# Attention and MLP on one core: weights loaded up to four pieces ahead, first loads dealt out over two queues, and every later q transposed by DMA

## The chip, the cores and the metric

The kernel runs on one core of a Trainium2 chip. The metric is device time in microseconds (us) for one execution; lower is better. The engines of the core are called PE (TensorE, matmul), PEld (its weight loads), DVE (VectorE), ACT (ScalarE), POOL (GpSimd) and SP (SyncE, which here only issues DMAs; "SPq" and "ACTq" are the queues on which SP and ACT issue them).

## The reference

```python
# q, k, v: (batch 8, heads 8, seq 576, head_dim 64) float32; tau = 0.02
scores = (q @ k.transpose(0, 1, 3, 2)) / sqrt(64)
scores = where(scores >= max(scores, -1) - tau, scores, -1e9)
attn   = softmax(scores, -1)
x      = (attn @ v).transpose(0, 2, 1, 3).reshape(4608, 512)
h      = x @ w_in            # w_in  512 x 2048
out    = (h - tanh(h)) @ w_out   # w_out 2048 x 512
```

## The kernel before

Heads are worked two at a time. There are 32 pairs, four for each of the 8 batches, and a pair has nine score tiles of 128 rows, so there are 288 tiles. The two heads have 576 rows each; eight tiles have 128 rows of one head, and one tile ("shared") has the last 64 rows of both heads.

Preparation of a pair. `load` (L138) brings k, q and v into `raw` tiles, two DMAs each, all issued on SP. `split` (L181), three POOL instructions (L184, L187, L188), scales a float32 tile and writes it as an fp16 high part and an fp16 low part into `hl`. `turn` (L243) transposes `hl`: nine PE transposes (L235) into a PSUM tile of the two-buffer pool `ps_big`, then one DVE copy (L258) to SBUF. For k, POOL also writes a copy with the two halves swapped (`kS`, L264). For q of some pairs, those for which `q_by_dma` (L239) is true, a DMA transpose issued on SP (L247) does this instead. Before the change these are the pairs from 8 on, except the first of each batch.

A tile. `scores` (L303) makes four matmuls (eight on the shared tile) into `ps_big`; DVE scales them and takes the row maximum (L336, L348); ACT writes `z`, which is zero or hugely negative (L363). Then `z` must be transposed. Up to pair 5 PE does it (L382); from pair 6 on, once per two tiles, a DMA transpose issued on SP does (L370, `zT<-z`). ACT takes the exponential (L391 or L399, `pT`), and PE multiplies with v (`attend`, L420, L427, L438). DVE normalizes, PE transposes the result (`emit_x`), and so the MLP's input `xT` is made.

The MLP of a batch (`layers`, L554) is cut into steps of four matmuls: `psH` (L493) for the first product and `psY` (L519) for the second. These steps are dealt out among the tiles of the next batch. The last batches' steps run alone at the end, from about 456 us on.

Weights. The two matrices come in 16 pieces of 512 KB. `w_load` (L629) issues a DMA on SP into a `wt` tile, and `w_cast` (L625) lets POOL write it as bf16 (L627). The pool `wt` has two buffers, so a load waits until the piece two before it has been cast.

Order. The program is written out by hand: one loop over steps `s`, in which scores run eight tiles ahead of `s`, `z` five tiles ahead, and `plan` holds at which step each preparation is put. Each engine, and SP's queue too, runs its own instructions in the order in which the loop wrote them. So an instruction that waits on SP holds up every DMA behind it. In `plan`, a pair whose q goes by DMA has its two splits two steps earlier (L663), and its q transpose seven steps before the pair's first scores, where the PE way has it two or three steps before (L665).

The start. `load_first` (L155) brings k and q of pair 0 in three DMAs each: first head, shared rows, second head. All of k goes on SP, all of q on ACT. `split_first` and `turn_first` work on the first head and the shared rows first (part 0), and on the second head after that (part 1).

Of the kernel before, what the change touches and what calls it, by code (L numbers as in the profile page):

```python
# [9 lines left out]
F32 = mybir.dt.float32  # L10
# [8 lines left out]
def kernel(  # L19
# [11 lines left out]
    nc = tc.nc  # L31
    P = 128

    B, H, S, D = q.shape
# [11 lines left out]
    HPAIR = H // 2  # L46
# [16 lines left out]
    AHEAD = 8  # L63
# [35 lines left out]
    for i in range(6):  # L99
# [8 lines left out]
    pool = lambda name, bufs, **kw: ctx.enter_context(  # L108
        tc.tile_pool(name=name, bufs=bufs, **kw)
    )  # L110
    PSUM = bass.MemoryType.PSUM
    raw_pool = pool("raw", 2)
# [5 lines left out]
    zt_pool = pool("zt", 6)  # L118
    p_pool = pool("p", 3)
    o_pool = pool("o", 2)  # L120
    wt_pool = pool("wt", 2)
    g_pool = pool("g", 2)
    t_pool = pool("t", 3)
    y_pool = pool("y", 2)
# [9 lines left out]
    raws = {}  # L134
# [17 lines left out]
        else:  # L152
            eng.dma_start(out=r[:, 4, :], in_=rem)

    def load_first(t, eng):  # L155

        src = {"k": k, "q": q}[t]
        r = raws[0, t] = raw_pool.tile([P, 10, D], F32, name=f"{t}raw", tag=t)
        for h in range(2):
            eng.dma_start(  # L160
                out=r[:, 5 * h : 5 * h + 4, :].rearrange("p c d -> p (c d)"),
                in_=src[0, h, 0:512, :].rearrange("(p c) d -> p (c d)", c=4),
            )
            if h == 0:
                rem = src[0, 0:2, 512:S, :].rearrange("h s d -> s h d")
                eng.dma_start(out=r[:, 4, :], in_=rem)

    load_first("k", nc.sync)
    load_first("q", nc.scalar)
    warm = const.tile([P, 1], F32, name="warm")  # L170
    nc.vector.memset(warm, 0.0)
    nc.scalar.activation(out=warm, in_=warm, func=ACT.Exp)
# [65 lines left out]

    def q_by_dma(p):  # L239

        return p >= 2 * HPAIR and p % 4 != 0

    def turn(p, t):  # L243
        hl = hls.pop((p, t))
# [58 lines left out]
    def scores(i):  # L303
        p, hh, t = place(i)
        qT, kT, kS = mats[p, "q"], mats[p, "k"], mats[p, "ks"]
        ps = ps_big.tile([P, 1024], F32, name="psS", tag="big")
        main, rem, lo = slice(0, 512), slice(512, 576), 0
        if kind(i) == "B":
            main, rem, lo = slice(512, 1024), slice(448, 512), 448
        if hh is None:  # L310
            qrem = REM
            if q_by_dma(p):
                qrem = (slice(512, 640, 2), slice(513, 640, 2))
            for n, kk in enumerate((kT, kS)):
                for dst, srcs in ((main, MAIN), (rem, REM)):
                    for hh in range(2):
                        nc.tensor.matmul(
                            out=ps[64 * hh : 64 * hh + 64, dst],
                            lhsT=qT[:, qrem[hh]], rhs=kk[:, srcs[hh]],
                            start=(n == 0), stop=(n == 1),  # L320
                        )
        else:
            lhs = qT[:, (5 * hh + t) * P : (5 * hh + t + 1) * P]
            for n, kk in enumerate((kT, kS)):
                for dst, src in ((main, MAIN[hh]), (rem, REM[hh])):
                    nc.tensor.matmul(  # L326
                        out=ps[:, dst], lhsT=lhs, rhs=kk[:, src],
                        start=(n == 0), stop=(n == 1),
                    )
        sc = sc_pool.tile([P, S], F32, name="sc")  # L330
        if kind(i) == "B":
            mx = mxs[i] = mxs.pop(i - 1)
        else:
            mx = mxs[i] = mx3[i // 2 % len(mx3)]
        c = int(kind(i) == "B")
        nc.vector.tensor_scalar(  # L336
            out=sc, in0=ps[:, lo : lo + S], scalar1=SC, scalar2=None,
            op0=ALU.mult, op1=ALU.max, accum_out=mx[:, c : c + 1],
        )
        scs[i] = sc  # L340

    def shift(i):

        if kind(i) == "A":
            return
        mx = mxs.pop(i)
        nb = st_pool.tile([P, 9], F32, name="nb", tag="nb")
        nc.vector.tensor_scalar(  # L348
            out=nb.rearrange("p (a b) -> p a b", b=3)[:, :, 0:2],
            in0=mx.rearrange("p (a b) -> p a b", b=4)[:, :, 0:3],  # L350
            scalar1=-1.0, scalar2=tau, op0=ALU.mult, op1=ALU.add,
        )
        nbs[i - 1], nbs[i] = nb[:, 0:1], nb[:, 1:2]
# [148 lines left out]
    def bend():  # L502
        while halves:
            m, n, ps = halves.pop(0)
            th = t_pool.tile([P, MB], F32, name="th")
            nc.scalar.activation(out=th, in_=ps, func=ACT.Tanh)  # L506
            ths.append((m, n, ps, th))

    def shrink():
        while ths:  # L510
            m, n, ps, th = ths.pop(0)
            nc.vector.scalar_tensor_tensor(  # L512
                out=gs[m][:, n, :], in0=th, scalar=-1.0, in1=ps,
                op0=ALU.mult, op1=ALU.add,
            )
# [98 lines left out]
    def w_pieces():  # L614
        for w, sb, n in ((moe_w_in, w_in_sb, DM_C), (moe_w_out, w_out_sb, DF_C)):
            flat = sb.rearrange("p c n -> p (c n)")
            cols = n * w.shape[1] // 8
            src = w.rearrange("(c p) n -> p c n", p=P)

            for i in (0, 2, 4, 6, 1, 3, 5, 7) if w is moe_w_in else range(8):  # L620
                yield flat, src, i, cols, w.shape[1]

    loaded = []

    def w_cast():  # L625
        flat, wt, i, cols = loaded.pop(0)
        nc.gpsimd.tensor_copy(out=flat[:, i * cols : (i + 1) * cols], in_=wt)  # L627

    def w_load(piece):  # L629
        flat, src, i, cols, width = piece  # L630
        wt = wt_pool.tile([P, cols], F32, name="wt", tag="wt")
        if cols >= width:
            r = cols // width
            s = src[:, i * r : (i + 1) * r, :]
            nc.sync.dma_start(out=wt.rearrange("p (c n) -> p c n", n=width), in_=s)
        else:
            r = width // cols
            s = src[:, i // r, (i % r) * cols : (i % r + 1) * cols]
            nc.sync.dma_start(out=wt, in_=s)
        loaded.append((flat, wt, i, cols))  # L640
# [13 lines left out]
    for p in range(1, NPAIR):  # L654
        first = TPP * p - AHEAD
        for d, f in PREP[3 if p == 1 else 0 :]:
            d -= p == 1 and d in (3, 5)
            if d in (7, 8) and q_by_dma(p):
                d = d + 2
            if p in (2, 4):  # L660
                d = {8: 9, 7: 8, 5: 6}.get(d, d)
            elif d == 5 and p >= 5:
                d = 6 if p % 2 else 3  # L663
            plan.setdefault(first - d, []).append(lambda p=p, f=f: f(p))
        d = 7 if q_by_dma(p) else 3 - (p == 1 or p >= 5)  # L665
        d = 4 if p in (2, 4) else d
# [10 lines left out]
    for t in ("k", "q", "v"):  # L677
        load(1, t)
    pieces = w_pieces()
    w_when = [3, 11, 19, 27] + [4 * i + 32 for i in range(4)] + [3 * i + 47 for i in range(9)]  # L680

    todo, stage = [], 0
    fold = const.tile([P, 64], BF16, name="fold")
# [13 lines left out]
    for s in range(-AHEAD, NTILE + LAG + 3):  # L697
        p, j = divmod(max(s, 0), TPP)
        if 0 <= s < NTILE and j == 2 + LAG and p % HPAIR == 0 and p >= HPAIR:
            assert not todo  # L700
            todo = layers(stage, False)
            share = len(todo) / (HPAIR * TPP - 2 - LAG)
            done, stage = 0.0, stage + 1
        if s == NTILE:
            todo = layers(stage, True)
            share, done, stage = 1, 0.0, stage + 1
        if 0 <= s + AHEAD - 1 < NTILE:
            shift(s + AHEAD - 1)
        if 0 <= s + AHEAD < NTILE:
            scores(s + AHEAD)  # L710
        if s == 1 - AHEAD:
            for t in ("k", "q", "ks"):
                turn_first(t, 1)
        for i in kinks.pop(s, []):
            kink(i)
        bend()
        for i in wts.pop(s, []):
            weights(i)
        if 0 <= s < NTILE + FIRST:
            if todo:  # L720
                done += share
                if s < NTILE and j == TPP - 1 and p % HPAIR == HPAIR - 1:
                    done = 1e9
                while todo and done >= 1:
                    todo.pop(0)()
                    done -= 1
        if s == 0:
            nc.vector.tensor_tensor(
                out=fold, in0=ident_bf[:, 0:64], in1=ident_bf[:, 64:P], op=ALU.add
            )  # L730
        shrink()
        for store in stores[:-1]:
            store()
        del stores[:-1]
        for i in atts.pop(s, []):
            pp, jj = divmod(i, TPP)
            if i < NTILE:
                attend(i)
                odd = pp % 2
                if jj == 3 + odd:  # L740
                    norm(pp, 0)
                elif odd and jj in (0, 8):
                    norm(pp - (jj == 0), 1)
            if pp and jj == 1 + pp % 2:
                emit_x(pp - 1)
        for step in plan.pop(s, []):
            step()
        if True:
            if s + AHEAD in w_when:
                if loaded:  # L750
                    w_cast()
                piece = next(pieces, None)
                if piece:
                    w_load(piece)

    for step in todo:
        step()
# [51 lines left out]
```

## Time and profile before

| What | us |
|---|---|
| Time, median of 6 runs (533.87 to 536.44) | 535.01 |
| The profiled execution's own time | 534.98 |
| Its span, first to last instruction | 533.2 |
| PE busy in the span | 510.2 (96%) |
| ACT busy | 435.4 (82%) |
| DVE busy | 420.5 (79%) |
| POOL busy | 289.7 (54%) |

Busy time is the time in which at least one instruction of that engine was running; an engine that waits is not busy. A share over the whole span hides that the stages differ: the first 100 us load the weights beside the attention, the middle is the same for each batch, and the last 75 us are matmuls alone. A DMA transpose issued on SP takes SP some 1.3 us to issue and lands a median of 3.3 us (`qT`) or 3.6 us (`zT`, 3.2 to 7.6) after its issue began.

### The profile page before, as it was taken

The numbers are of one execution on the slowest core, as the hardware profiler recorded it, in microseconds if no ns is written. First come the engines' busy times: TensorE is split into PE (matmuls) and PEld (weight loads), VectorE is DVE, ScalarE is ACT, GpSimd is POOL, SyncE is SP. The second block draws the span as 40 slices with busy tenths as digits, with TensorE's granted clock in tenths as the row PEclk, the third lists the DMA queues.
The fourth block names the chain that finished last, engine by engine and source line by source line (L and its number), as shares of the span: only waits on it lengthen the run. The fifth ranks groups of instructions, "written<-read, shape, count | busy, mean of one in ns | idle before, by whom it ended". The sixth has DMA issues, their size and how long they took to land.

```text
span 533.2 us, 12716 instructions
## 1 busy us (share of the span) xinstructions
PE 510.2 (96%) x4606; PEld 287.8 (54%) x4606; DVE 420.5 (79%) x1179; ACT 435.4 (82%) x617; POOL 289.7 (54%) x390
## 2 busy tenths in 40 slices
PE   8999899987999999999999999999999999999996
PEld 4666566554556555555555555655555555444444
DVE  5899879995888988898889988898889887554440
ACT  5999899987898999889898989898889999543330
POOL 7999987773755757475727574575747530000000
PEclk9999999997999999999999999999999999999999
DMA  7462767989997999899998899899989996400113
GB/s 202 146 191 88 223 197 146 223 172 192 175 200 158 188 190 203 189 177 199 186 212 170 186 195 193 175 180 196 209 185 178 201 152 109 105 28 33 39 39 81
DMA packets 208607, 86.79 MB, mean 163 GB/s; under 512 B 176160, under 2 KB 200992, under 8 KB 208544
## 3 DMA queue, kind: packets, MB, share of 16 engines
q1 hardware_dynamic: 207952, 85.56, 76.1%
q8 instruction: 36, 0.59, 0.5%
q10 hardware_dynamic: 592, 0.43, 0.3%
q14 instruction: 27, 0.22, 0.1%
HBM read 36.70 MB, written 9.44 MB: 87 GB/s over the span
## 4 chain that ended last, share of the span: by engine, by line
PE 35%; issue 19%; POOL 19%; ACT 10%; DMA 9%; DVE 5%; SPq 2%; POOLq 0%; ACTq 0%; DVEq 0%
PE psY L519 12%; PE psH L493 9%; PE psS L326 6%; POOL kS L264 5%; ACT z L363 4%; ACT pT L391 3%; DMA vraw<-in_v_dram 3%; POOL khl L188 3%; DMA kraw<-in_k_dram 3%; PE psHt L493 3%; DMA zT<-z 2%; POOL vb L216 2%; ACT pT L399 2%; PE psO L427 1%; POOL kraw L184 1%
## 5 line engine op out<-in xcount | busy, mean ns | idle before, releaser
L336 DVE TENSOR_SCALAR_CACHE_REDUCE sc<-psS 128x576 f32<-128x576 f32 x288 | 214.0, 752 | 40.8 <-PE psS L326 24.5
L363 ACT ACTIVATE z<-sc,nb 128x576 bf16<-128x576 f32 x288 | 215.6, 769 | 21.6 <-DVE nb L348 19.4
L399 ACT ACTIVATE pT<-zT 128x1152 f16<-128x1152 bf16 x117 | 135.0, 1154 | 15.3 <-DMA zT<-z 15.2
L519 PE MATMUL psY<-w_out_sb,g 128*128 128x512 bf16 (+1 forms) x592 | 146.3, 374 | 0.8 <-DVE yo L532 0.8
L264 POOL COPY kS<-kT 64x1152 f16<-64x1152 f16 x62 | 70.8, 1142 | 117.6 <-DVE nb L348 115.9
L493 PE MATMUL psH<-xT,w_in_sb 128*128 128x512 bf16 x480 | 124.2, 381 | 2.3 <-DVE g L512 2.3
L326 PEld LDWEIGHTS <-qT 128*128 128x128 f16 x1024 | 75.0, 98 | 61.9 <-issue 7.8
L326 PE MATMUL psS<-kT,qT 128*128 128x512 f16 (+1 forms) x512 | 104.9, 286 | 3.0 <-DVE sc L336 1.5
L326 PE MATMUL psS<-kS,qT 128*128 128x512 f16 x496 | 101.9, 287 | 1.6 <-POOL kS L264 1.5
L512 DVE SCALAR_TENSOR_TENSOR g<-th,psH 128x512 bf16<-128x512 f32 x128 | 87.5, 683 | 19.7 <-ACT th L506 19.1
L506 ACT ACTIVATE th<-psH 128x512 f32<-128x512 f32 x128 | 74.6, 583 | 22.3 <-PE psH L493 21.8
L519 PEld LDWEIGHTS <-g 128*128 128x128 bf16 x592 | 51.1, 98 | 57.3 <-issue 3.2
L493 PEld LDWEIGHTS <-w_in_sb 128*128 128x128 bf16 x576 | 49.3, 98 | 57.5 <-issue 5.5
L427 PE MATMUL psO<-vb,pT 128*128 128x65 bf16 x1024 | 53.5, 194 | 0.0
L427 PEld LDWEIGHTS <-pT 128*128 128x128 f16 x1024 | 44.4, 98 | 9.7
L188 POOL TENSOR_TENSOR qhl<-qraw,qhl 128x576 f16<-128x576 f32 x31 | 39.7, 1279 | 2.7
L188 POOL TENSOR_TENSOR khl<-kraw,khl 128x576 f16<-128x576 f32 x31 | 39.6, 1278 | 2.7
L391 ACT ACTIVATE pT<-psZ 128x512 f16<-128x512 bf16 (+1 forms) x54 | 35.1, 653 | 3.9 <-PE psZ L382 3.6
L532 DVE COPY yo<-psY 128x512 f32<-128x512 f32 (+1 forms) x31 | 21.1, 682 | 14.4 <-PE psY L519 12.7
L420 PE MATMUL psO<-vb,pT 128*128 128x130 bf16 x128 | 28.3, 221 | 4.2 <-ACT pT L399 3.5
L453 DVE TENSOR_TENSOR osb<-psO,rc 128x256 bf16<-128x256 f32 x64 | 27.2, 424 | 2.2
L258 DVE COPY kT<-ps_k 128x1152 f16<-128x1152 f16 x31 | 23.3, 751 | 4.1 <-PE ps_k L235 4.1
(79 smaller groups left out, 507.6 us busy)
## 6 DMA issues: line engine op xcount, KB each, us to landing
vraw<-in_v_dram SPq DMA_DIRECT2D x32, 256.0 KB, 4.2
out_dram<-yo SPq DMA_DIRECT2D x32, 256.0 KB, 2.8
kraw<-in_k_dram SPq DMA_DIRECT2D x31, 256.0 KB, 3.1
qraw<-in_q_dram SPq DMA_DIRECT2D x31, 256.0 KB, 3.6
wt<-in_moe_w_in_dram SPq DMA_DIRECT2D x8, 512.0 KB, 4.3
wt<-in_moe_w_out_dram SPq DMA_DIRECT2D x8, 512.0 KB, 4.7
zT<-z SPq DMA_TRANSPOSE x117, 3.6
kraw<-in_k_dram SPq DMA_DIRECT2D x32, 32.0 KB, 2.9
```

The costliest lines, as they stand in the source:

```text
L188: nc.gpsimd.tensor_tensor(out=hl[:, :, 1, :], in0=x, in1=hl[:, :, 0, :], op=ALU.subtract)
L264: nc.gpsimd.tensor_copy(out=o, in_=i)
L326: nc.tensor.matmul(out=ps[:, dst], lhsT=lhs, rhs=kk[:, src], start=(n == 0), stop=(n == 1),)
L336: nc.vector.tensor_scalar(out=sc, in0=ps[:, lo : lo + S], scalar1=SC, scalar2=None, op0=ALU.mult, op1=ALU.max, accum_out=mx[:, c : c + 1],)
L363: nc.scalar.activation(out=z, in_=sc, func=ACT.Prelu, bias=nb, scale=1.0, alpha=STEEP)
L391: nc.scalar.activation(out=pt[:, off * P : (off + n) * P], in_=ps[:, 0 : n * P], func=ACT.Exp)
L399: nc.scalar.activation(out=pt[:, 0 : n * P], in_=zts.pop(i)[:, 0:n, :], func=ACT.Exp)
L427: nc.tensor.matmul(out=po[:, t - 1 + ab, :], lhsT=pt[:, blk * P : (blk + 1) * P], rhs=vb[:, hh, c, :], start=False, stop=(n == 7), skip_gr ...
L493: nc.tensor.matmul(out=ps, lhsT=w_in_sb[:, c, n * P : (n + 1) * P], rhs=xs[m][:, c, :] if m < B else xR[:, c, :, :], start=(c == 0), stop= ...
L506: nc.scalar.activation(out=th, in_=ps, func=ACT.Tanh)
L512: nc.vector.scalar_tensor_tensor(out=gs[m][:, n, :], in0=th, scalar=-1.0, in1=ps, op0=ALU.mult, op1=ALU.add,)
L519: nc.tensor.matmul(out=ps, lhsT=gs[m][:, n, ms * P : (ms + 1) * P], rhs=w_out_sb[:, n, cols], start=(n == 0), stop=(n == DF_C - 1),)
```

## The change

There are three edits. The pool `wt` gets four buffers, and the steps at which a piece is loaded are separated from those at which one is cast: the casts stay where they were, and the loads come up to four pieces ahead of them. The loads of pair 0 are dealt out over SP and ACT in another order: SP issues k's first head, q's shared rows and k's second head; ACT issues k's shared rows, q's first head and q's second head. And `q_by_dma` is true for every pair from 8 on, so that q of pairs 8, 12, 16, 20, 24 and 28 goes by DMA too; with that, `plan` puts their splits two steps earlier and their transposes five steps earlier than the PE way had it.

```diff
-    wt_pool = pool("wt", 2)
+    wt_pool = pool("wt", 4)
...
-    def load_first(t, eng):
+    def load_first(t, h, eng):
 
         src = {"k": k, "q": q}[t]
-        r = raws[0, t] = raw_pool.tile([P, 10, D], F32, name=f"{t}raw", tag=t)
-        for h in range(2):
+        if (0, t) not in raws:
+            raws[0, t] = raw_pool.tile([P, 10, D], F32, name=f"{t}raw", tag=t)
+        r = raws[0, t]
+        if h is None:
+            rem = src[0, 0:2, 512:S, :].rearrange("h s d -> s h d")
+            eng.dma_start(out=r[:, 4, :], in_=rem)
+        else:
             eng.dma_start(
                 out=r[:, 5 * h : 5 * h + 4, :].rearrange("p c d -> p (c d)"),
                 in_=src[0, h, 0:512, :].rearrange("(p c) d -> p (c d)", c=4),
             )
-            if h == 0:
-                rem = src[0, 0:2, 512:S, :].rearrange("h s d -> s h d")
-                eng.dma_start(out=r[:, 4, :], in_=rem)
-
-    load_first("k", nc.sync)
-    load_first("q", nc.scalar)
+
+
+    for t, h in (("k", 0), ("q", None), ("k", 1)):
+        load_first(t, h, nc.sync)
+    for t, h in (("k", None), ("q", 0), ("q", 1)):
+        load_first(t, h, nc.scalar)
...
     def q_by_dma(p):
 
-        return p >= 2 * HPAIR and p % 4 != 0
+        return p >= 2 * HPAIR
...
-    w_when = [3, 11, 19, 27] + [4 * i + 32 for i in range(4)] + [3 * i + 47 for i in range(9)]
+    load_when = [3, 8, 13, 18, 21, 25, 29, 34, 38, 42, 46, 49, 52, 55, 58, 61]
+    cast_when = [11, 19, 27] + [4 * i + 32 for i in range(3)] + [3 * i + 44 for i in range(10)]
...
-        if True:
-            if s + AHEAD in w_when:
-                if loaded:
-                    w_cast()
-                piece = next(pieces, None)
-                if piece:
-                    w_load(piece)
+        if s + AHEAD in cast_when:
+            w_cast()
+        if s + AHEAD in load_when:
+            w_load(next(pieces))
```

## The prediction, made before the changed kernel was run

> **What bounds the kernel now.** I read the page's busy totals first, and then the table of stretches, for totals hide that stages differ. Its columns: stretch, length, busy time of PE, PEld, DVE, ACT and POOL (instructions in brackets), granted PE clock, DMA share, GB/s.
>
> ```profile
> 115.00:118.00 3.00, 3.00 (x41) 1.65 (x39) 2.13 (x8) 2.93 (x4) 2.06 (x4) 1.00 0.94 196
> 118.00:121.00 3.00, 1.11 (x8) 0.44 (x6) 2.38 (x9) 0.00 (x0) 2.57 (x3) 1.00 1.00 201
> 121.00:124.00 3.00, 1.35 (x15) 1.16 (x16) 0.11 (x1) 2.49 (x3) 2.69 (x5) 0.54 1.03 150
> 124.00:128.00 4.00, 4.00 (x14) 1.53 (x13) 1.67 (x6) 2.95 (x5) 1.06 (x3) 0.50 1.12 223
> ...
> 220.76:278.30 57.54, 56.67 (x518) 31.71 (x517) 50.29 (x144) 52.09 (x70) 34.33 (x45) 1.00 0.95 190
> 278.30:335.77 57.47, 56.60 (x518) 31.71 (x517) 50.30 (x144) 52.00 (x70) 34.36 (x45) 1.00 0.93 188
> ```
>
> Two things are to be seen. A batch in the middle takes 57.5 us, and PE is busy for 56.6 of it, ACT for 52 and DVE for 50: PE sets the pace there. And at 118 us PE stands still, after which its granted clock is 0.50 for a while (the clock record gives 6.83 us, from 121.27 to 128.10). It is the only PE gap over 0.8 us in the span. I followed it back through the timeline of each engine (start, length, engine, line, what, and in brackets the idle time before it with what ended that).
>
> ```profile
> 101.46 1.04 POOL L627 CAST w_out_sb<-wt 128x1024 bf16<-128x1024 f32 x1 [2.63 <-DMA wt<-in_moe_w_out_dram]
> ...
> 109.76 1.04 POOL L627 CAST w_out_sb<-wt 128x1024 bf16<-128x1024 f32 x1 [2.02 <-DMA wt<-in_moe_w_out_dram]
> ...
> 112.25 1.28 POOL L188 TENSOR_TENSOR qhl<-qraw,qhl 128x576 f16<-128x576 f32 x1
> ```
> ```profile
> 113.56 1.28 SPq L247 DMA_TRANSPOSE qT<-qhl  x1
> ...
> 117.40 1.76 SPq L370 DMA_TRANSPOSE zT<-z  x1
> ```
> ```profile
> 121.43 1.16 ACT L399 ACTIVATE pT<-zT 128x1152 f16<-128x1152 bf16 x1 [3.50 <-DMA zT<-z]
> ```
> ```profile
> 122.65 0.29 PE L420 MATMUL psO<-vb,pT 128*128 128x130 bf16 x1 [3.50 <-ACT pT L399]
> ```
>
> POOL waits 2.02 us for the last weight piece, so the split of pair 9's q ends only at 113.53. SP had been free since 111.1 and waits for it, with four k and q loads and a `zT` behind it. The `z` for that `zT` was finished at 112.49; its transpose is issued at 117.40, 4.9 us late, lands at 121.32, and ACT and PE wait 3.50 us each.
>
> **The change part by part.**
>
> *Weight loads ahead.* The 16 DMAs and 16 casts stay; only their place on SP moves. Before, the last four pieces were issued at 85.8, 90.8, 96.4 and 102.4 us among the first `zT`; three casts waited for them (1.87, 2.63 and 2.02 us). A load now waits for the cast four pieces back, and the casts end, by the trace, at 76.7, 83.1, 88.3 for the last three loads. So the last piece is issued near 88.4 and lands by 93 to 96 (4.1 to 7.3 us from issue, by the rows of the old last four), before the first of the last three casts matters. What follows on POOL: the swap of pair 8's k (L264) cannot start before its DVE copy, done at 102.05, so of the earlier waits only 0.46 us is gained there (102.56 to 102.1). Then k's split, the cast without its 2.02 us, and q's split follow by their own lengths: q's split ends at 113.53 - 0.46 - 2.02 = 111.05. SP then issues the same things as before, 2.48 us earlier: the `zT` at 114.9, landing after the same 3.92 us at 118.8, the exponential 1.16 us, PE from about 120.1 instead of 122.65. That is 2.55 us.
>
> The other half is the clock. PE ran from 122.65 to 128.10 at half clock, 5.45 us for 2.72 us' worth of matmuls, so 2.72 us are lost. The clock fell 2.1 us after PE's last work had ended (119.15 to 121.27). The stall that is left, from 119.15 to 120.1 or from about a microsecond earlier (q of pair 8 is gone from PE), is 1 to 2 us. I take it that the clock stays: gain 2.55 + 2.72 = 5.27. Bounds: nothing, if the `zT` is as late as before; and all, 3.50 + 2.72 = 6.22.
>
> The Trainium skill, "TensorE: Matmul & The Clock Gate", Part 1, says that the clock is halved after an idle window of about 3.4 us, windows that run freely and do not start with the gap. The row above has it falling 2.1 us into a gap, which a free-running window allows only if a partly busy one counts as idle. By the rule a remaining gap of 1 to 2 us keeps the clock; by the row it is close, and I leave a rival for it.
>
> What the moved loads hold up: SP waits for casts at new places, with the loads of k, q and v behind. The latest ones are q of pair 5, issued near 43.9 instead of 36.0, wanted by POOL at 54.6, and k of pair 8, near 77.2 instead of 72.2, wanted at 91.2. A load lands in 3 to 4.5 us, so some 6 us are left: cost nothing; without that cover each microsecond of POOL would be one of the path, as POOL is busy 9.4 of each 10 us there.
>
> *Pair 0's loads.* By the landing records, k's first head came at 3.25 and its shared rows, second on SP, at 4.54; ACT's first split started at 4.62. With the shared rows first on ACT it may start when ACT's warm-up ends, 3.99: up to 0.63 us. But the first `z` also follows part 1, whose POOL chain (5.06 to 8.80) starts with k's second head, landed 4.99, third on SP before and after; PE's next step waits for its end at 8.80. Cover gone, 0.63; I take 0.1, bounds 0 and 0.63.
>
> *q of pairs 8, 12, ... 28 by DMA.* Removed: six times nine PE transposes and a DVE copy (756 ns). On PE the nine stand between an MLP step and the next scores:
>
> ```profile
> 277.68 1.03 PE L493 MATMUL psH<-xT,w_in_sb 128*128 128x512 bf16 x4
> 278.54 0.67 PE L235 MATMUL ps_q<-ident_f,qhl 128*128 128x128 f16 x9
> 279.04 0.41 PE L326 MATMUL psS<-kT,qT 128*128 128x512 f16 x2
> ```
>
> From 278.54 to 279.04 PE does nothing else, and the same 0.50 us is there for pairs 12, 16, 24 and 28. As PE sets the pace, this is 5 x 0.50 = 2.5 us. Pair 8's comes before the stall and is swallowed by it (PE waits for the same `pT`): nothing; if the stall were gone, 0.43 us of waiting and 0.74 us of work. The DVE copies lie beside PE, which has the later end (50 of 57.5 us): nothing. Bounds: 2.5 + 1.17 = 3.7 above; 0 below, if ACT (52 of 57.5) or SP takes over.
>
> Added: six DMA transposes, 1.31 us of SP each and 288 KB, in front of a k load, and the `zT` behind them. q's split is done by then (267.94, and SP comes to that place at 270.5). What must not be late is the `zT` right after. The exponential of the two next `zT` starts later than they land by 4.7 and 3.3 us for pair 12, 4.1 and 2.3 for pair 16, 4.1 and 2.6 for pair 20, 3.7 and 2.0 for pair 24, 4.0 and 2.1 for pair 28. All exceed 1.31: nothing. For pair 8, SP comes there at about 94.5 and waits some 0.4 us for POOL, with k of pair 9 (wanted at 104.5) behind; the weight issues that stood there are gone.
>
> The Trainium skill, "VectorE: DVE Perf Modes", in its rules for kernel authors, speaks against this edit: transpose 128x128 on TensorE when the result may go to PSUM, by DMA otherwise; its table has 390 against 1309 ns a block. By these figures a pair would lose 9 x 0.92 = 8.3 us and the six pairs 50 us, an estimate, and the change would be slower by some 44 us. The rows price what sets the end: 0.50 us of PE against an SP and a DMA with room, the whole `qT` landing 3.3 us after issue.
>
> **Sum.** 0.1 + 5.3 + 2.5 = 7.9 us. The profiled execution took 534.98 us (533.2 span and 1.8 around it), 0.03 under the median, so 527.1. Everything at its best is 0.63 + 6.22 + 3.7 = 10.5: 524.5.
>
> **The rivals.**
>
> *The clock still falls.* For it: it fell 2.1 us into the gap, and 1 to 2 us remain. Against: no other gap (all under 0.8 us) made it fall. Then 2.72 us are not won, 529.8; if the `zT` is also as late as before, only 2.6 us are won, 532.4. Middle 531.
>
> *PE's work is not the price.* ACT at 52 of 57.5 us or SP's order binds where q was; several exponentials in a batch already start within 0.1 us of their `zT`'s landing. Against: at the places where q stood the landing is 4 us ahead. Time 534.98 - 5.4 = 529.6.
>
> *Slower: the added transposes make the `zT` behind them late.* One mechanism, at pairs 12 to 28. `zT` landing times go up to 7.6 us where DMAs pile up, and the DMA share is 0.95 already. At the tightest place (`zT` issued at 333.99, landed 338.30, wanted 340.28, 1.98 us of room) an issue 1.31 us later and a landing of 7.6 instead of 4.3 us make 4.6 - 2.0 = 2.6 us of stall a batch, 5 x 2.6 = 13 against 7.9 won: 540.1. It decides from a lateness of 1.98 + 7.9 / 5 = 3.6 us on. Against: the other three pairs of each batch already do the same, at busier places.
>
> *No change that can be told*, because a new wait eats all: nothing speaks for one of that very size.
>
> **How the numbers follow.** Chances: forecast 0.62 (its own range 524.5 to 529.3), clock 0.20, PE not the price 0.06, slower 0.09, no change 0.03. This kernel's runs tell a difference from about 0.2% on, 1.1 us. Faster 0.62 + 0.20 + 0.06 = 0.88, same 0.03, slower 0.09. The range, 524.5 to 532.0, takes in the forecast with its bounds and most of the first two rivals, and leaves out the slower one.
>
> **What would show it.** Right: no POOL wait on `wt`; the gap at 118 us under 2 us and a clock of 1.00 throughout; batches from 163 us on of 57.0 instead of 57.5 us; 141 DMA transposes, 54 PE transposes fewer. Wrong: a second PE gap over 2 us with a clock of 0.5; SP waiting for q's split of pair 8, 12 and so on; exponentials behind the added transposes that wait for `zT`; batches of 57.5 us in spite of the missing transposes.

## The result: slower by 0.3%, and the profile after

| | before | after |
|---|---|---|
| Median (us) | 535.38 (533.23 to 537.80, 73 runs) | 537.17 (534.74 to 538.53, 36 runs) |
| Ratio after / before, 95% interval | | 1.0032 (1.0024 to 1.0041) |
| Profiled execution, span (us) | 533.2 | 535.6 |
| First `z` of batch 3 (tile 108) starts at | 171.16 | 168.05 |
| From there to the end of the span | 362.0 | 367.6 |

The last two rows split the matter, in the one profiled execution of each kernel. Up to tile 108 the changed kernel won 3.1 us, and from there it lost 5.6. (Line numbers of the changed file are higher by five: `zT` is issued in L375, ACT's exponential is L404.)

*The first part went as foretold in kind.* POOL's timeline (start, length, engine, line, what; a bracket would name a wait) shows the last three casts without a wait for a weight piece, and q's split of pair 9 ending at 109.47 + 1.28 = 110.75 us instead of 113.53:

```profile
94.39 1.04 POOL L632 CAST w_out_sb<-wt 128x1024 bf16<-128x1024 f32 x1
...
96.64 1.04 POOL L632 CAST w_out_sb<-wt 128x1024 bf16<-128x1024 f32 x1
...
106.97 1.04 POOL L632 CAST w_out_sb<-wt 128x1024 bf16<-128x1024 f32 x1
...
109.47 1.28 POOL L193 TENSOR_TENSOR qhl<-qraw,qhl 128x576 f16<-128x576 f32 x1
```

The stall of 3.50 us on PE has become smaller ones, two of them here (PE's timeline), and in the table of stretches (columns as in the prediction) the granted clock, after the last bracketed count, is 1.00 in every row:

```profile
119.69 0.23 PE L425 MATMUL psO<-vb,pT 128*128 128x130 bf16 x1 [0.78 <-ACT pT L404]
...
124.59 0.23 PE L425 MATMUL psO<-vb,pT 128*128 128x130 bf16 x1 [1.46 <-ACT pT L404]
```
```profile
118.00:121.00 3.00, 2.19 (x26) 1.27 (x25) 2.67 (x12) 2.50 (x3) 2.85 (x4) 1.00 1.75 186
121.00:124.00 3.00, 2.13 (x12) 0.81 (x10) 2.27 (x7) 0.63 (x1) 1.69 (x4) 1.00 0.66 143
124.00:128.00 4.00, 3.41 (x32) 1.78 (x33) 1.59 (x5) 4.00 (x7) 0.00 (x0) 1.00 1.02 219
```

*The loss is in the middle of each batch.* A batch has 36 tiles; the stretches below are its thirds, from the `z` of its first, 13th and 25th tile, for batch 4. The kernel before, then the changed one:

```profile
228.34:245.50 17.16, 16.99 (x170) 9.71 (x168) 15.74 (x48) 16.57 (x23) 9.99 (x15) 1.00 1.04 191
245.50:264.65 19.15, 18.77 (x171) 10.59 (x170) 16.98 (x48) 17.57 (x25) 12.95 (x16) 1.00 0.96 199
264.65:285.88 21.23, 20.91 (x182) 11.41 (x181) 17.57 (x50) 17.95 (x25) 11.39 (x15) 1.00 0.93 178
```
```profile
226.54:243.33 16.79, 16.62 (x168) 9.57 (x166) 15.73 (x48) 16.45 (x22) 10.29 (x15) 1.00 0.91 179
243.33:264.62 21.29, 19.39 (x173) 10.78 (x171) 17.14 (x48) 17.58 (x26) 12.94 (x16) 1.00 0.96 192
264.62:285.52 20.90, 20.53 (x173) 10.96 (x171) 16.87 (x49) 17.95 (x26) 11.10 (x15) 1.00 1.04 194
```

The last third, where q's nine PE transposes stood, is 0.33 us shorter. The middle third, in which the change moves nothing, is 2.14 us longer. In batches 3 to 7 it takes 20.81, 21.28, 20.15, 20.72 and 21.07 us, against 19.16 to 19.34 before: 8.0 us in all.

What waits there? ACT's timeline, before and after, at the same tile of batch 4:

```profile
251.94 0.60 ACT L506 ACTIVATE th<-psH 128x512 f32<-128x512 f32 x1
253.71 1.16 ACT L399 ACTIVATE pT<-zT 128x1152 f16<-128x1152 bf16 x1 [1.18 <-DMA zT<-z]
```
```profile
249.77 0.60 ACT L511 ACTIVATE th<-psH 128x512 f32<-128x512 f32 x1
253.79 1.16 ACT L404 ACTIVATE pT<-zT 128x1152 f16<-128x1152 bf16 x1 [3.42 <-DMA zT<-z]
```

The exponential waits 3.42 us for a `zT` instead of 1.18. This wait was there before the change: SP sends four `zT` one after the other, behind six loads, an earlier `zT` and a store, and the first of them releases ACT 0.1 us after it lands. It had no slack. SP's queue, before and after:

```profile
248.12 0.64 SPq L151 DMA_DIRECT2D vraw<-in_v_dram  x1
248.86 8.01 SPq L370 DMA_TRANSPOSE zT<-z  x4
256.97 1.31 SPq L247 DMA_TRANSPOSE qT<-qhl  x1
```
```profile
247.32 0.64 SPq L151 DMA_DIRECT2D vraw<-in_v_dram  x1
248.06 8.86 SPq L375 DMA_TRANSPOSE zT<-z  x4
257.03 1.35 SPq L252 DMA_TRANSPOSE qT<-qhl  x1
```

The same transposes stand in the same order, with no added one among them, yet the four take 8.86 us to issue instead of 8.01, and the first lands 5.7 us after its issue instead of 4.8. Counted from the batch's first `z` it lands at 27.2 us instead of 25.3; 1.0 of these 1.9 us is a later issue (21.5 instead of 20.5). A later issue alone does no harm: a kernel further down issues it at 21.3 us and has it landed at 24.9. So something else takes the DMA's time. The page's list of DMA queues (packets, MB, share) has a row that I had not read, here before and after:

```profile
q8 instruction: 36, 0.59, 0.5%
```
```profile
q8 instruction: 35, 0.57, 0.4%
```

36 packets of 16 KB are 0.59 MB. The page lists 9,212 instructions for PE and PEld together before and 9,104 after; spread over them, the packets come to 64 bytes each, before and (within one packet) after. So I read these packets as PE's program, fetched piece by piece as it runs, 256 instructions a piece. One takes 1.1 us on average. The change takes 18 of PE's instructions (nine transposes and their weight loads) out of each batch. Four fetches are 1024 instructions; a batch in the middle had 1035 in the table of stretches (518 matmuls, 517 weight loads) and has 18 fewer now. Before, the places of the fetches drifted: the one nearest to the four `zT` came 22.1 us after the batch's first `z` in batch 3 and 18.5 us in batch 7. After, they fall on nearly the same places in every batch: about 12.3, 24.3, 40.5 and 55.4 us. The one at 24.3 us (23.4 to 24.7) falls on the four `zT`.

The Trainium skill, "Advanced Engine Details and Errata", section "ISA Cache", gives a cache line of 16 KB, which is 256 instructions; the packets here agree with it. "DMA: Bandwidth & Descriptors", section "Queues, rings and completion order", says that a DMA engine finishes a whole packet of one queue before it turns to the next, which, if the page's packets are the profile's, would let one such packet hold up the transposes' packets behind it; the trace does not list packets by engine, so no run here shows that.

### The profile page after: what moved, and what is told of

It is laid out like the page before. It is cut to its first block, busy times and chain, and to the rows that moved or that the text cites. A ratio compares the mean times of both kernels' runs of the same rounds, so it can differ in the third digit from the quotient of the medians.

```text
span 535.6 us, 12603 instructions
## 1 busy us (share of the span) xinstructions
PE 507.4 (95%) x4552; PEld 284.3 (53%) x4552; DVE 417.1 (78%) x1173; ACT 435.0 (81%) x617; POOL 289.2 (54%) x390
## 4 chain that ended last, share of the span: by engine, by line
PE 35%; ACT 23%; issue 17%; DMA 11%; POOL 7%; DVE 5%; SPq 1%; ACTq 0%; POOLq 0%; DVEq 0%
PE psY L524 12%; ACT z L368 10%; PE psH L498 9%; DMA zT<-z 7%; ACT pT L404 6%; PE psS L331 6%; ACT th L511 3%; ACT pT L396 3%; DMA vraw<-in_v_dram 3%; POOL kS L269 3%; PE psHt L498 3%; DMA kraw<-in_k_dram 2%; PE psO L432 1%; DVE sc L341 1%; DVE kT L263 1%
## 5 line engine op out<-in xcount | busy, mean ns | idle before, releaser
L404 ACT ACTIVATE pT<-zT 128x1152 f16<-128x1152 bf16 x117 | 135.0, 1154 | 20.5 <-DMA zT<-z 20.5
L458 DVE TENSOR_TENSOR osb<-psO,rc 128x256 bf16<-128x256 f32 x64 | 27.2, 424 | 2.2
L263 DVE COPY kT<-ps_k 128x1152 f16<-128x1152 f16 x31 | 23.3, 751 | 4.1 <-PE ps_k L240 4.1
```

The source lines that it names most:

```text
L404: nc.scalar.activation(out=pt[:, 0 : n * P], in_=zts.pop(i)[:, 0:n, :], func=ACT.Exp)
```

## The experiments

Theory F: the fetches of PE's program fall on `zT` transposes that have no slack; the change moved them there. Theory S, the rival: the added q transposes themselves load SP and the DMA engines. Medians and spans of all runs stand in one table at the end of this section; its last three columns are of the one profiled execution of each kernel.

**1. Each edit by itself.** Without the q edit (the first kernel), and the kernel before with the q edit alone (the second, the same line the other way round):

```diff
-        return p >= 2 * HPAIR
+        return p >= 2 * HPAIR and p % 4 != 0
```

> The change without its third edit: weight loads ahead and pair 0's loads dealt out, q of the first pair of a batch still on PE. Both theories expect the stall at 118 us to shrink as in the changed kernel and the middle third of each batch (tiles 12 to 24 of its 36, by the starts of z) to stay at 19.2 us, so about 3 us less than before: 532.4 us. If the middle third grows to 20.7 here too, the q edit is not what costs the time.

> The kernel before with the q edit alone. Both theories expect the stall at 118 us to stay and the middle third of batches 3 to 7 to grow from 19.2 to 20.2 to 21.3 us each, as in the changed kernel: about 540 us. About 532.5 (the 2.5 us of the prediction) would mean that the loss needs the moved weight loads.

Without it 533.22 us, with it alone 539.3. So the loss belongs to the q edit, and the other two edits gain 0.4%. Without the q edit the middle thirds stay at 19.2 to 19.8 us. With it alone only two of the five grew in the profiled execution (21.16 and 20.79 us), fewer than expected; in two other batches the first third grew instead (17.63 and 18.02 us, against 16.79 to 17.15 before). This doesn't tell F from S.

**2. More PE instructions in the changed kernel.** One or two tiny matmuls (a weight load and a matmul each) for each of 32 tiles of the first batch, 64 or 128 instructions, their results overwritten; every added DMA transpose stays.

```diff
+        if 4 <= i < 36:
+            for _ in range(2):
+                nc.tensor.matmul(
+                    out=ps[0:16, 0:8], lhsT=ident_f16[:, 0:16], rhs=ident_f16[:, 0:8],
+                    start=True, stop=True,
+                )
```

> The changed kernel plus 64 PE instructions: one weight load and one 8-column matmul more on each of tiles 4 to 35, where PE has room; their results are not used. Theory F: PE's program is fetched in 16 KB pieces by DMA, 18 instructions fewer a batch have moved these fetches to 12.3 and 24.3 us after a batch's start, where they delay the z transposes that have no room; 64 instructions (a quarter of a piece) move them some 3.6 us earlier, as they lie in the kernel before, and the middle third goes back to 19.2 us: 537.2 - 8 = 529.2 us. Theory S: the added q transposes themselves make SP and the DMAs late; the padding changes nothing: 537.2 us.

> The changed kernel plus 128 PE instructions (two small matmuls on each of tiles 4 to 35; results not used). Theory F: the fetches lie about 5, 17, 33 and 48 us after a batch's start, as in the last batch of the kernel before, and the middle third is 19.2 us: 529.2 us. Theory S: 537.2 us, as without the padding.

534.11 and 533.15 us: more work for PE made the kernel 3 to 4 us faster. S said 537.2. F's 529.2 was missed too. From tile 108 on the loss is gone (361.9 and 362.2 us instead of 367.6), but the small matmuls cost 2.5 and 3.2 us where they stand (the `z` of tile 36 starts at 57.29 and 57.92 us instead of 54.76), and the 8 us were the middle thirds alone, where the kernel had lost 5.6 net.

**3. The same without cost, and the other way round.** The warm-up matmuls at the start (L182) run from 1.2 us on, before PE's first transposes at 5.4. A few large ones were replaced by many small ones, so that more instructions pass in about the same time. Once in the changed kernel (shown; 48 matmuls more, which are 96 instructions; the expectation says 90), once in the kernel before (1 large and 106 small ones, 192 instructions more); the third kernel puts the 18 instructions back into each batch of the changed one, and the fourth is the kernel before with the earlier weight loads alone.

```diff
-    for n in range(11):
+    for n in range(3):
         nc.tensor.matmul(out=pz, lhsT=zero[:, 0:P], rhs=zero, start=True, stop=True)
+    for n in range(56):
+        nc.tensor.matmul(
+            out=pz[0:16, 0:64], lhsT=zero[:, 0:16], rhs=zero[:, 0:64],
+            start=True, stop=True,
+        )
```
```diff
+        if i >= 71 and i % 36 == 35 and i < 288 - 36:
+            for _ in range(9):
+                nc.tensor.matmul(
+                    out=ps[0:16, 0:8], lhsT=ident_f16[:, 0:16], rhs=ident_f16[:, 0:8],
+                    start=True, stop=True,
+                )
```

> The changed kernel with 90 more TensorE instructions in the warm-up before the first transposes (56 small matmuls in place of 8 large ones), so that the batches hold nothing that the changed kernel does not. Theory F (the fetches of TensorE's program, 16 KB each, fall on transposes of z that have no slack): the fetches move some 5 us earlier in every batch, the middle thirds of batches 3 to 7 go from 20.2 to 21.3 us back to 19.2 to 19.6, and 537.2 less 8.0 for these and plus up to 1 for what the fetches hit instead gives 529.2 to 530.2 us. Theory S (the added transposes of q themselves load SP and the DMA engines): nothing changes in the batches, 537.2.

> The kernel before with 192 more TensorE instructions in the warm-up (106 small matmuls in place of 10 large ones), and nothing else. F: 192 of the 256 instructions of a fetch shift the fetches by three quarters of 13.8 us, so that those of batch 3 come 12 to 13 us after its start instead of 8.9, drifting to 8 or 9 by batch 7: batches 3 to 5 fall into the place where the changed kernel lost 1 to 2 us each, 535.4 plus 3 to 5 gives 538.4 to 540.4. S: no transposes are added, 535.4.

> The changed kernel with nine small matmuls (18 instructions) put at the end of each of the batches 2 to 7, so that TensorE's program has as many instructions as before the change. F: the fetches drift through the batches as before, the middle thirds are 19.2 us; 537.2 less 8.0, plus 54 small matmuls at the 0.045 us that they cost with 64 of them early on (2.4 us) gives 531.6. S: 537.2 to 539.6.

> The kernel before with the earlier weight loads alone. Both theories: the kernel without the q edit (533.2) less the head's 0.33 us, 533.5; the waits of POOL on weight pieces gone, the gap at 118 us shorter than 3.5 us. Under F the number of TensorE's instructions is as before, so the middle thirds stay at 19.2 us.

The changed kernel with 96 more takes 530.0 us, 0.9915 (0.989 to 0.994) of before: the loss is gone, though all 141 DMA transposes are there. With 18 put back in each batch it takes 532.23. The kernel before with 192 more is the plainest: nothing of the change is in it, and its batch 4 shows the changed kernel's loss. Its stretches of the middle and last third, and the exponential there (lines as in the changed file):

```profile
243.56:264.56 21.00, 19.23 (x170) 10.79 (x171) 17.14 (x48) 17.57 (x26) 12.93 (x16) 1.00 0.95 195
264.56:285.76 21.20, 20.72 (x179) 11.40 (x180) 17.54 (x50) 18.05 (x26) 11.41 (x15) 1.00 0.94 182
```
```profile
253.74 1.16 ACT L404 ACTIVATE pT<-zT 128x1152 f16<-128x1152 bf16 x1 [3.14 <-DMA zT<-z]
```

From tile 108 on it takes 365.7 us instead of 362.0, 3.7 more, inside the 3 to 5 expected. The total was not: its median, 535.92, rose by 1.0 us only and lies below the 538.4 to 540.4 expected. The profiled execution reached tile 108 1.9 us earlier, which I had not foreseen; its stall near 120 us is 2.26 us instead of 3.50, and its half clock 3.41 us instead of 6.83.

The changed kernel with 96 more has its four `zT` through in 6.85 us at the same place (SP's queue; line numbers higher by another five), and its middle third is as before:

```profile
246.16 6.85 SPq L380 DMA_TRANSPOSE zT<-z  x4
```
```profile
241.69:260.85 19.16, 18.70 (x170) 10.71 (x171) 16.98 (x48) 17.59 (x25) 12.95 (x16) 1.00 0.91 202
```

**4. The dose.** If a fetch is 256 instructions, 192 more must also clear the place, and 256 more must bring the loss back. Both are the changed kernel, with 1 large matmul and 106 small ones of 40 columns, or 138 of 24. The third is the kernel before with the new order of pair 0's loads alone.

> The changed kernel with 256 more TensorE instructions in the warm-up (138 small matmuls in place of 10 large ones): a whole fetch of 16 KB more. F: the phase comes back to that of the changed kernel, fetches some 12 and 24 us after the start of batches 3 to 7, middle thirds of 20.2 to 21.3 us again, and the gain of the version with 90 more (530.0) is lost: 535.5 to 537.5 us. Rival W (the small matmuls in the warm-up help in some other way, by the clock or by an earlier start): it stays near 530.

> The changed kernel with 192 more TensorE instructions in the warm-up (106 small matmuls in place of 10 large ones), the number that made batches 4 and 5 of the kernel before longer by some 1.5 us each. F: three quarters of a fetch bring the fetches from 12.3 and 24.3 us to about 1.5, 13.5 and 30 us after a batch's start, none between 23.4 and 25 us: middle thirds 19.2 to 19.6 us and 529.5 to 531.5 us. A rival by which more instructions in the warm-up are bad or good as such would give 537 or more, or the same as with 256.

> The kernel before with the new order of the first pair's loads alone. Both theories: the first z starts 0.3 to 0.4 us earlier, the waits of POOL on weight pieces and the gap of 3.5 us at 118 us stay, TensorE's instructions are as many as before: 535.4 less 0.33 gives 535.1, a difference that the measurement hardly resolves.

With 192 more 530.33 us, with 256 more 536.37: the loss came back, as F said. The middle third of batch 5 with 256 more, and of batch 4 with 192:

```profile
300.89:321.78 20.89, 19.22 (x170) 10.78 (x171) 17.12 (x48) 17.56 (x25) 12.93 (x16) 1.00 0.94 196
```
```profile
240.24:259.40 19.16, 18.70 (x170) 10.71 (x171) 16.97 (x48) 17.58 (x26) 12.95 (x16) 1.00 0.99 212
```

Batch 4 in four doses of the changed kernel (us after the batch's first `z`; from the trace's DMA records):

| more instructions in the warm-up | fetches near the four `zT` | first `zT` lands | middle third |
|---|---|---|---|
| 0 | 12.3, 24.7 | 27.2 | 21.28 |
| 96 | 18.6 | 24.9 | 19.16 |
| 192 | 14.4, 27.8 | 24.9 | 19.16 |
| 256 | 12.5, 23.9 | 26.1 | 20.24 |

Over batches 3 to 7 of all 13 profiles: in 17 batches a fetch began between 23.3 and 25.0 us, and there the first `zT` landed 5.3 us after its issue on average; in the 48 others 4.2 us. The middle third averages 20.50 and 19.33 us. Of the 17, three lost nothing or little (19.16, 19.16, 19.54): in two of them that `zT` had been sent early, at 20.5 and 20.8 us, and landed at 24.4 and 25.0, about as the fetch began; in the last the batch's first third was 1.2 us longer instead. The fetch at 12 us, which comes with the one at 24, does not do it alone: in the kernel before with 192 more, batch 3 has one at 12.0 us and the next at 26.4, and in the kernel before with the q edit, batch 7 has one at 12.3 and the next just as the `zT` lands; their middle thirds are 19.50 and 19.16 us. Other places may cost something too: the three batches with a fetch at 10.3 to 10.5 us have first thirds of 17.6 to 18.2 us.

| kernel | median (us) | ratio to before, 95% | span | to tile 108 | from tile 108 |
|---|---|---|---|---|---|
| changed, no q edit | 533.22 | 0.9963 (0.9945 to 0.9982) | 530.6 | 168.6 | 362.0 |
| before + q edit | 539.3 | 1.0083 (1.0054 to 1.0111) | 536.2 | 170.6 | 365.6 |
| before + weight loads ahead | 534.03 | 0.9981 (0.9963 to 0.9999) | 531.3 | 168.9 | 362.4 |
| before + pair 0's order | 533.76 | 0.9977 (0.9962 to 0.9993) | 530.2 | 168.5 | 361.7 |
| before + 192 in warm-up | 535.92 | 1.0026 (1.0007 to 1.0045) | 535.0 | 169.3 | 365.7 |
| changed + 64 in batch 0 | 534.11 | 0.9983 (0.9963 to 1.0003) | 532.3 | 170.4 | 361.9 |
| changed + 128 in batch 0 | 533.15 | 0.9974 (0.9953 to 0.9996) | 531.6 | 169.4 | 362.2 |
| changed + 18 a batch | 532.23 | 0.9951 (0.9933 to 0.9970) | 531.2 | 168.5 | 362.7 |
| changed + 96 in warm-up | 530.0 | 0.9915 (0.9890 to 0.9940) | 528.4 | 167.8 | 360.6 |
| changed + 192 in warm-up | 530.33 | 0.9900 (0.9881 to 0.9918) | 527.2 | 166.0 | 361.3 |
| changed + 256 in warm-up | 536.37 | 1.0014 (0.9997 to 1.0031) | 535.4 | 167.8 | 367.5 |

## Why the prediction was wrong, by its own steps

*Weight loads ahead: the waits right, the gain mis-sized.* POOL's waits went, and q's split ended at 110.75 us (111.05 foretold, less the 0.33 by which everything starts earlier). The later loads of k, q and v held nothing up, as foretold, though loads in that stretch of the kernel before (51 to 100 us) landed in 2.6 to 7.4 us, not 3 to 4.5. The 5.27 us were made of 2.55 for a shorter stall and 2.72 for the clock. The clock term came, 2.72. The stall term did not: gaps of 0.90 (at 108.72), 0.78 and 1.46 add up to 3.14 against 3.50. From tile 68 to tile 108 the changed kernel won 2.8 us (65.6 against 68.4), and some 0.3 of these belong to pair 12's q. I followed the one `zT` that was late and did not ask which comes next.

Nor do the weight loads alone decide the clock. Without the q edit it still falls for 3.41 us in the profiled execution (a stall of 2.81 us), and only 1 of 12 executions has a mean granted clock of 0.998 or more; with the weight loads alone 3 of 12 do, with the q edit alone all six, and the kernel before with nothing but 192 more instructions in the warm-up 11 of 12. What decides it was not followed up. The clock term was also sized on one execution: of the 76 executions of the kernel before that were run beside the experiments, 40 have a mean clock of 0.994 or less, as the profiled one, 18 have 0.997, and 5 have 0.998 or more; the times average 535.6 us at 0.994, 534.1 at 0.997 and 533.4 in those five. By themselves the earlier weight loads are worth 1.0 us (0.9981, interval 0.9963 to 0.9999), not 5.3.

*Pair 0's loads: mis-sized.* 0.1 us taken, 0 to 0.63 bounded. In the profiled execution the first `z` starts 0.40 us earlier (9.95 against 10.35), and 0.33 of it lasts to tile 68. Over the 13 profiles it starts at 9.73 to 10.30 us with the new order and at 10.35 to 10.78 without, 0.68 us apart on average, and at tile 68 (the two kernels with matmuls added in the first batch left out) it is still 0.7 us: the gain lies at the upper bound. Alone the edit gave 0.9977, 1.2 us; in its profiled execution the stall at 118 us is also shorter, 2.75 us with 3.41 us of half clock instead of 3.50 and 6.83. How an earlier start would do that was not followed up.

*q by DMA: the step that failed.* The working took 2.5 us of PE for what is removed and "nothing" for what is added. The five places gave about 0.3 us each, not 0.50 (last thirds of 20.9 against 21.2), 1.6 us in all. Four of them stand behind tile 108; with the fetches elsewhere, the stretch from there to the end is 0.7 to 1.4 us shorter than before (361.3 and 360.6 against 362.0), about what they are worth. What I costed at nothing and what cost the time is neither the transposes added nor the time removed: it is that PE's *program* became 18 instructions a batch shorter. That pinned the fetches to one place of every batch, and cost 5.6 us net. The lower bound of 0 rested on ACT and SP alone; the DMA engines' own timetable was not in the sum. The prediction did note that several exponentials start within 0.1 us of their `zT`'s landing, but asked for the slack of those behind the added transposes alone.

*The rivals.* "Slower" had the right sign and the wrong place: it put the lateness behind the added transposes, at pairs 12 to 28, where the last thirds in fact got shorter. Theory S, the same thought, was refuted by the kernels that keep every added transpose and run at 530. "The clock still falls" did not happen in the profiled execution, nor, by a mean clock of 0.998 or more, in 36 of all 37.

*The signs named in advance.* No POOL wait for `wt`, gaps under 2 us, a clock of 1.00, 141 DMA transposes and 54 PE transposes fewer: all came. Batches of 57.0 us did not: 58.49, 58.97, 57.84 and 58.41 us. That sign was the telling one, and thirds of a batch placed it.

*What stays open.* In the 17 batches the fetch takes 0.9 to 1.6 us, while the first `zT` lands up to 2 us late; how one packet costs more than its own length was not shown. The kernel before with 96 more instructions in the warm-up was not run, so what the change is worth with the fetches at like places is known only from its parts, and part of the 530 may be the stall at 118 us, whose longest gap comes out between 1.16 and 3.50 us from kernel to kernel.

## What to carry to other kernels

This kernel fetched PE's program by DMA all through its 535 us, beside its data, and adding or removing PE instructions shifted every later fetch. Where a loop's length in instructions is near a whole number of fetches, a collision can repeat in every round: list the fetch packets beside the transfers that have no slack, before costing an edit. If an edit that saves work makes the kernel slower in a place that it does not touch, shift the phase with instructions in idle time (here the warm-up: 537.2 to 530.0 us) before judging it.

## What the runs showed of the hardware

- Each packet of the instruction queue q8 is 16 KB and takes 1.1 us on average. A DMA transpose that overlaps one in its issue takes SP 2.01 us on average instead of 1.43 (kernel before, 26 against 109 transposes), and over 2 us in 46% of cases instead of 1%; in the changed kernel it is 1.84 instead of 1.44.
- 256 more PE instructions brought the loss back that 96 and 192 had removed: the period is that of one packet, 256 instructions of 64 bytes.
- The half clock comes in steps of 3.41 us (3.41 or 6.83 us long). The full clock before it lasted 116.05 us in six of the profiles, 34 of these steps, wherever the gap lay, and 119.47 us, 35 steps, in a seventh. It fell at gaps of 2.19 to 3.50 us, and stayed at gaps up to 1.84 us; one gap of 2.53 us left it full. Counted in these steps, the one that ends as the clock falls holds 2.1 to 2.8 us without a matmul in all seven, while the gap of 2.53 us (119.04 to 121.57, full clock since 6.94) lies across an end of a step at 119.58, with 0.54 us before it and 1.99 after. The Trainium skill, "TensorE: Matmul & The Clock Gate", Part 1, asks for an idle window of about 3.4 us, free-running; the steps agree, but here a window that was idle for 2.1 of its 3.41 us was enough.
